# Three low parts of the first key's w1 go from GpSimd to VectorE, and the first tile's transposes all go inside the convolution (routed feed-forward, one core)

## Chip, cores and metric

The kernel runs on one core of a Trainium2 chip. The metric is the device time of one execution in microseconds (us). The time before is 1267.22 us, the median of three runs (1266.97 to 1270.43). The trace is of one further execution, profiled.

## What is computed

A causal seven-tap convolution with softmaxed taps is taken along the sequence for each head; its 28672 rows are then routed to eight experts. The routing is greedy over all (token, expert) logits in falling order, 3584 rows to an expert. Each expert is a feed-forward layer.

```python
w = softmax(weight)                              # 8 heads x 7 taps
x = conv(x_pad, w)                               # 28672 x 192, head by head
logits = x @ w_gate                              # 28672 x 8
assigned = greedy(logits, cap=3584)              # highest logits first
for e in range(8):
    h = maximum(x[assigned == e] @ w1[e], 0)     # w1: 192 x 1024
    out[assigned == e] = h @ w2[e]               # w2: 1024 x 192
```

## The kernel before

**Precision.** The matrix products of the feed-forward use a reduced float32 (`FR`) in two parts. A value is split into a high part, which ScalarE (ACT) copies, and a low part, the value less its high part, which a second engine subtracts. This holds for the weights (`wsplit`, L1208), for the transposed rows (`evac`, L1280) and for the hidden layer (`l1`, L1290: `hh` is high, `hl` is low).

**Convolution.** `moe_kernel` (L1420) loops over 16 blocks `i` of 1792 rows and, inside `k.conv` (L195), over eight heads `h`. The text calls one round of the inner loop step i.h; the planner's counter is `at = 8 * i + h`. Each step issues the convolution's matmuls for one head into one of four PSUM banks, then calls `mid(h)` (L1565), then lets ACT copy the bank into the block's tile `a`. After head 7 ACT's queue issues the store of the block to `attn` (L204). Inside `mid` a list `left` is worked off: VectorE transposes of the block before (`k.transp`, tile `aT`) and the gate's matmuls of the block before that (`gate`, then `end`, which ends in a maximum on VectorE, tile `M1`, printed as `M`). The gate needs all four transposes of its block.

**The first key.** A key is one expert's set of weights. From step 14.1 on, every odd step splits one piece of the first key's w1: a0 at 14.1, d0 at 14.3, a1 at 14.5, d1 at 14.7. A piece `a` is 128 x 512, a piece `d` is 64 x 512 (its load is two DMAs). `wsplit` has ACT make the high part, has the engine it is given make the low part, and then queues on SyncE (SP), in this order: a store of the high part (`kw`), a store of the low part (`kw` or `kd`, L1252), and the load of the piece four places further on (`wload`, L1190, tile `raw`). Four `raw` buffers circulate. The pieces behind d1 are the four w2 pieces of the first key, split in tile 0 of the feed-forward at f = 0 to 3, and a0, d0, a1, d1 of the second key, split at f = 4 to 7; their low parts are VectorE's.

**The first fetches.** When the first half of the routing is done, `hook` (L1539) calls `first()`, which queues on GpSimd (POOL) a memset and four indirect gathers for tile 0 and the same for tile 1 (`gather`, L1257, tile `xg`), and notes the step in `got`. From then on `mid` takes two items of `left` a step.

**The first tile's transposes.** `todo` (L1532) holds four items: the four TensorE transposes of tile 0's first 128 columns (u0) and their split into `xa`, then the four of the last 64 columns (u1) and their split into `xd`. `hook` takes two items in a step where `at >= got[0] + 10 and at % 8 in (2, 5)`; what is left is done behind the loop (L1589), ahead of the VectorE transposes of block 15 (L1591).

**Feed-forward.** `FFN.run` (L1384) goes through tiles of 512 rows. Per f, `l1` issues five matmuls into one of three banks `ph`; the first three read `xa`, the last two `xd`; ACT then writes `hh` and VectorE `hl`. Behind l1 of tile 0 stand, by `at(1)` (L1622), the gates and ends of blocks 14 and 15 (tile `bg` at this point), whose bias copies (`L`) are on ACT behind the last split of tile 0. Then tile 1 begins. Each engine takes its instructions in the order of the program; the order comes from a planner that adds up modelled engine times (`Pace`, L60).

```python
A.activation(hi, r, AF.Copy)
eng.tensor_tensor(lo, r[0:n], hi[0:n].bitcast(F32), op=OP.subtract)
...
S.dma_start(self.kept1[e][:, 2, s], hi.bitcast(F32))
S.dma_start(self.keptd[e][:, s], lo.bitcast(F32))
...
self.wload()
```

Of the kernel before, what the change touches and what calls it, by code (L numbers as in the profile page):

```python
# [1419 lines left out]
def moe_kernel(ctx, tc, x, weight, wg, w1, w2, out):  # L1420
    nc = Pace(tc.nc)
    V, P = nc.vector, nc.gpsimd
# [4 lines left out]
    with ExitStack() as cw:  # L1427
# [11 lines left out]
        ff = FFN(tc, nc, attn, w1, w2, out, r.ident, wr, drm)  # L1439
# [87 lines left out]
        def first():  # L1527
            for e in range(2):
                ff.gather(e, [ja0[:, e, b:b + 1] for b in range(4)], NTOK // 2, P)


        todo = [partial(f, 0, *a) for u in range(2) for f, a in ((lambda i, u: ff.transp(i, u, r.bg()), (u,)), (ff.evac, (u,)))]  # L1532
        got, left = [], []
# [5 lines left out]
        def hook(at):  # L1539
            nc.pe = max(nc.pe, PERIOD * at / 8 + START)  # L1540
            bg.hook(1.5)
            if not got and len(bg.gens) == 4:
                first()
                got.append(at)
            elif got and at >= got[0] + 10 and at % 8 in (2, 5) and todo:
                for _ in range(2):
                    todo.pop(0)()

# [5 lines left out]
        for i in range(NHB):  # L1554
            if i + 3 < NHB:
                k.load(i + 3)
            if i == 4:
                r.consts_late()
            if i == 13:
                cx[0].close()  # L1560
                for _ in range(4):
                    ff.wload()
                ff.wpool(cw, 0, **late)

            def mid(h):  # L1565

                if i and h == 0:
                    for u in range(4):
                        left.append(partial(k.transp, i - 1, u))
                        if i > 1:  # L1570
                            left.append(partial(gate, i - 2, u) if u < 3 else partial(end, i - 2))
                for _ in range(2 if got else 1):
                    if left and (i < LAG or got):
                        left.pop(0)()
                if i >= 14 and h % 2:
                    ff.wsplit(-1, P)
                hook(8 * i + h)

            k.conv(i, mid)
# [82 lines left out]
```

## Time and profile before

| what | value |
|---|---|
| median of three runs | 1267.22 us |
| profiled execution, its own time | 1268.0 us |
| span of the profiled execution | 1266.2 us |
| TensorE matmul (PE) busy | 1222.0 us, 97% of the span |
| VectorE (DVE) busy | 999.6 us, 79% |
| ACT busy | 551.2 us, 44% |
| POOL busy | 510.1 us, 40% |
| mean granted TensorE clock | 0.994 |

Times in the rows are us from the start of the span, durations of one instruction ns where the view says so. PEld is TensorE's weight load. SPq and ACTq are the DMA queues of SyncE and ScalarE. Most compute instructions show the one line L55, that of a helper, and are told apart by their tiles. A granted clock of 1.00 is 2.4 GHz, 0.50 is 1.2 GHz.

### The profile page before, as it was taken

What the parts mean: (1) busy time and instruction counts of PE and PEld (TensorE: products, weight loads), DVE (VectorE), ACT (ScalarE), POOL (GpSimd) and SP (SyncE); (2) the same over time, 40 slices, a digit from 0 to 9 for tenths busy, and PEclk for the clock granted to TensorE, in tenths of its full rate; (3) what the DMA queues carried; (4) which work ended last, traced back from release to release, by engine and by line L of the source; (5) the groups of instructions that cost most, each with busy time, mean ns of one, the idle gap of its engine ahead of it and who ended that gap; (6) DMA issues with size and microseconds to landing.
All of it is one profiled execution on the core that took longest, in us unless ns stands there. A gap on an engine that the chain in (4) does not pass through costs nothing.

```text
span 1266.2 us, 21792 instructions
## 1 busy us (share of the span) xinstructions
PE 1222.0 (97%) x7839; PEld 1049.9 (83%) x7839; DVE 999.6 (79%) x2245; ACT 551.2 (44%) x1220; POOL 510.1 (40%) x504
## 2 busy tenths in 40 slices
PE   5889979999999999999999999999999999999997
PEld 2445558899889888887889999999999999999997
DVE  7398669999999989988857777777777777777772
ACT  4544645565544543643433333333333333333332
POOL 3000435364444443533244444444444444444422
PEclk9999989999999999999999999999999999999999
DMA  9999897999533343423653513242314132231100
GB/s 236 347 334 297 271 328 257 294 316 319 194 103 112 122 152 94 152 93 125 161 126 105 205 41 100 94 155 62 129 48 147 46 102 97 85 105 47 45 26 28
DMA packets 100579, 193.02 MB, mean 152 GB/s; under 512 B 19232, under 2 KB 64752, under 8 KB 96240
## 3 DMA queue, kind: packets, MB, share of 16 engines
q1 hardware_dynamic: 57856, 115.15, 28.1%
q0 software_dynamic: 21504, 44.07, 11.7%
q10 hardware_dynamic: 21104, 32.34, 7.8%
q8 instruction: 63, 1.03, 0.3%
q14 instruction: 52, 0.43, 0.1%
HBM read 116.02 MB, written 75.50 MB: 151 GB/s over the span
## 4 chain that ended last, share of the span: by engine, by line
PE 83%; DVE 7%; DMA 5%; issue 1%; POOL 1%; ACT 1%; SPq 1%; POOLq 0%; ACTq 0%; DVEq 0%
PE ph L55 38%; PE y L55 37%; PE cv L55 3%; PE bg L55 3%; DMA X<-in_x_dram 1%; PE px L55 1%; DVE X L55 1%; DMA raw<-in_moe_w_dram 1%; DVE hl L55 1%; DVE oa L55 1%; DVE aT L55 1%; DMA wgr<-in_moe_w_gate_dram 1%; PE pl L55 1%; DMA X<-otab 1%; POOL xg L1262 0%
## 5 line engine op out<-in xcount | busy, mean ns | idle before, releaser
L55 PE MATMUL y<-w,hh 128*128 128x384 f32 x1792 | 539.3, 356 | 0.0
L55 ACT ACTIVATE hh<-ph 128x512 fp32r<-128x512 f32 x448 | 268.1, 598 | 494.2 <-PE ph L55 493.9
L55 PE MATMUL y<-w,hl 128*128 128x192 f32 x1792 | 448.9, 251 | 0.0
L55 DVE SCALAR_TENSOR_TENSOR hl<-ph,hh 128x512 fp32r<-128x512 f32 x448 | 308.1, 688 | 140.6 <-ACT hh L55 136.6
L55 PE MATMUL ph<-xa,w 128*128 128x512 f32 x1344 | 395.7, 402 | 3.9 <-DVE hl L55 3.9
L55 PEld LDWEIGHTS y<-w,hl 128*128 128x128 f32 x1792 | 341.0, 190 | 15.1
L55 PEld LDWEIGHTS y<-w,hh 128*128 128x128 f32 x1792 | 336.4, 188 | 19.1 <-issue 2.3
L1337 POOL DMA_INDIRECT out_dram<-yo,ib x128 | 127.9, 999 | 288.4 <-DVE yo L55 278.6
L55 PEld LDWEIGHTS ph<-xa,w 128*128 128x128 f32 x1344 | 218.7, 189 | 24.6 <-DVE hl L55 5.2
L1337 POOL DMA_INDIRECT out_dram<-yo,ia x96 | 112.2, 1168 | 262.3 <-DVE yo L55 230.0
L55 DVE STREAM_TRANSPOSE xs<-xg 32x256 f32<-32x256 f32 x496 | 182.9, 369 | 8.5
L55 PE MATMUL ph<-xd,w 128*128 128x512 f32 x448 | 177.3, 396 | 1.5 <-DVE xd L55 1.5
L55 PE MATMUL ph<-xd,dl 128*128 128x512 f32 x448 | 174.5, 390 | 0.0
L1262 POOL DMA_INDIRECT xg<-attn,jb x128 | 137.8, 1076 | 40.9 <-issue 40.9
L1262 POOL DMA_INDIRECT xg<-attn,ja x96 | 110.2, 1147 | 32.1 <-issue 26.7
L55 ACT ACTIVATE yt<-y 128x192 f32<-128x192 f32 x224 | 73.6, 328 | 102.6 <-PE y L55 99.5
L55 PE MATMUL cv<-X,TH 118*128 118x384 f32 x256 | 99.6, 515 | 18.9 <-DVE TH L55 12.5
L55 DVE TENSOR_TENSOR yo<-y,yt 128x192 f32<-128x192 f32 x224 | 79.4, 354 | 40.8 <-ACT yt L55 38.1
L55 PEld LDWEIGHTS ph<-xd,w 128*128 128x128 f32 x448 | 84.2, 188 | 21.2 <-DVE xd L55 2.0
L55 PEld LDWEIGHTS ph<-xd,dl 128*128 128x128 f32 x448 | 84.3, 188 | 19.7
L55 PEld LDWEIGHTS cv<-X,TH 118*128 118x128 f32 x256 | 44.6, 194 | 51.8 <-issue 13.0
L55 ACT ACTIVATE a<-cv 128x384 f32<-128x384 f32 x128 | 59.7, 492 | 53.3 <-PE cv L55 32.0
(237 smaller groups left out, 900.4 us busy)
## 6 DMA issues: line engine op xcount, KB each, us to landing
w<-kw SPq DMA_DIRECT2D x16, 1536.0 KB
w<-kv SPq DMA_DIRECT2D x16, 1536.0 KB
attn<-a ACTq DMA_DIRECT2D x16, 1344.0 KB
kw<-w SPq DMA_DIRECT2D x48, 256.0 KB
kv<-w SPq DMA_DIRECT2D x32, 384.0 KB
X<-in_x_dram SPq DMA_DIRECT2D x17, 672.0 KB
X<-in_x_dram ACTq DMA_DIRECT2D x15, 672.0 KB
raw<-in_moe_w_dram SPq DMA_DIRECT2D x32, 192.0 KB
```

The costliest lines, as they stand in the source:

```text
L55: return f(*a, **k)
L1262: self.nc.gpsimd.indirect_dma_start(out=t[:, b], out_offset=None, in_=self.attn[0:rows], in_offset=bass.IndirectOffsetOnAxis(ap=idx[b], ax ...
L1337: st = self.nc.gpsimd.indirect_dma_start(out=self.out, out_offset=bass.IndirectOffsetOnAxis(ap=idx, axis=0), in_=o, in_offset=None, bounds ...
```

## The change

The low parts of the first key's w1 are made by VectorE where the first fetches have already been queued, and by GpSimd otherwise. The condition for taking two items of `todo` becomes: at least 11 steps behind `got`, and an even counter.

```diff
@@ -1542,7 +1542,7 @@
             if not got and len(bg.gens) == 4:
                 first()
                 got.append(at)
-            elif got and at >= got[0] + 10 and at % 8 in (2, 5) and todo:
+            elif got and at >= got[0] + 11 and at % 2 == 0 and todo:
                 for _ in range(2):
                     todo.pop(0)()
 
@@ -1573,7 +1573,7 @@
                     if left and (i < LAG or got):
                         left.pop(0)()
                 if i >= 14 and h % 2:
-                    ff.wsplit(-1, P)
+                    ff.wsplit(-1, V if got else P)
                 hook(8 * i + h)
```

## Rows read from the trace of the kernel before

**Rows 1.** Page, part 1, busy time of TensorE (first of its lines)
```profile
PE 1222.0 (97%) x7839; PEld 1049.9 (83%) x7839; DVE 999.6 (79%) x2245; ACT 551.2 (44%) x1220; POOL 510.1 (40%) x504
```

**Rows 2.** Waits of TensorE from 185 us to the end, the longest kind: total, times, longest
```profile
PE bg L55 <- DVE c_bi L55: 2.0, 3, 1.0
```

**Rows 3.** Windows of 5 us; columns: length, busy PE, PEld, DVE, ACT, POOL, PEclk, DMA share, GB/s
```profile
155.00:160.00 5.00, 4.04 (x22) 2.43 (x18) 1.42 (x4) 3.46 (x9) 4.88 (x5) 1.00 0.55 159
160.00:165.00 5.00, 3.74 (x17) 2.84 (x18) 4.97 (x7) 2.95 (x6) 3.97 (x4) 1.00 1.00 304
...
175.00:180.00 5.00, 4.09 (x52) 2.73 (x50) 4.42 (x7) 3.57 (x7) 0.00 (x0) 0.50 1.03 384
```

**Rows 4.** Chain that ended last, 155 to 185 us: start, length, what
```profile
155.22 1.29 POOL dl L1243
...
174.15 5.30 DMA raw<-in_moe_w_dram
...
180.47 3.21 PE bg L55 x49
...
184.51 1.26 PE ph L55 x5
```

**Rows 5.** Waits of SP's queue, 100 to 215 us: total, times, longest
```profile
SPq L1252 <- POOL dl L1243: 9.6, 1, 9.6
```

**Rows 6.** Timeline of SP's queue: start, length, line, transfer
```profile
156.53 0.47 SPq L1252 DMA_DIRECT2D kd<-dl  x1
157.06 0.58 SPq L1203 DMA_DIRECT2D raw<-in_moe_w_dram  x1
...
162.53 2.54 SPq L1203 DMA_DIRECT2D raw<-in_moe_w_dram  x1
```

**Rows 7.** Timeline of ACT, 160 to 175 us: the idle time before and its releaser in brackets
```profile
168.29 0.53 ACT L55 ACTIVATE w<-raw 128x384 fp32r<-128x384 f32 x1 [3.13 <-DMA raw<-in_moe_w_dram]
...
172.09 0.52 ACT L55 ACTIVATE w<-raw 128x384 fp32r<-128x384 f32 x1 [2.78 <-DMA raw<-in_moe_w_dram]
```

**Rows 8.** Timeline of POOL, 140 to 175 us
```profile
141.82 1.28 POOL L1243 TENSOR_TENSOR w<-raw,w 128x512 fp32r<-128x512 f32 x1 [33.04 <-ACT w L55]
...
148.26 1.00 POOL L1262 DMA_INDIRECT xg<-attn,ja  x1 [0.30 <-issue]
...
172.26 1.00 POOL L1262 DMA_INDIRECT xg<-attn,ja  x1 [0.30 <-issue]
```

**Rows 9.** Instructions on tile raw, 100 to 190 us: min/median/max ns, first and last start
```profile
L55 DVE TENSOR_TENSOR dl<-raw,w x2: 683/683/683, 176.9 to 180.1; 64x512 fp32r<-64x512 f32 x2
```

**Rows 10.** Timeline of DVE, 150 to 175 us
```profile
151.33 0.38 DVE L55 TENSOR_REDUCE M<-LT 128x16 f32<-128x128 f32 x1 [1.17 <-ACT LT L55]
...
160.54 3.56 DVE L55 STREAM_TRANSPOSE aT<-a 128x768 f32<-128x768 f32 x4
...
172.64 0.56 DVE L55 TENSOR_TENSOR w<-raw,w 128x384 fp32r<-128x384 f32 x1 [2.61 <-ACT w L55]
```

**Rows 11.** Timeline of TensorE's weight loads, 154 to 157 us
```profile
154.97 0.30 PEld L55 LDWEIGHTS cv<-X,TH 118*128 118x128 f32 x2 [0.20 <-issue]
...
156.28 0.14 PEld L55 LDWEIGHTS bg<-ident,xg 128*128 128x128 f32 x1 [0.20 <-DMA xg<-attn,ja]
```

**Rows 12.** Tile xg, 100 to 200 us, last line: its 16 gathers from issue to landing
```profile
DMA to landing us min/median/max: 4.0/6.9/10.0
```

**Rows 13.** Timeline of TensorE, 156 to 176 us
```profile
156.45 1.46 PE L55 MATMUL cv<-X,TH 118*128 118x384 f32 x4
157.74 0.60 PE L55 MATMUL bg<-ident,xg 128*64 128x128 f32 x4
...
173.87 1.65 PE L55 MATMUL ph<-xa,w 128*128 128x512 f32 x3 [2.36 <-DVE hl L55]
```

**Rows 14.** Windows of 1 us around the change of clock; columns as in the windows of 5 us
```profile
173.00:174.00 1.00, 0.13 (x1) 0.13 (x1) 0.82 (x2) 0.09 (x1) 0.27 (x1) 0.61 0.93 348
...
183.00:184.00 1.00, 0.62 (x16) 0.20 (x4) 0.00 (x0) 0.30 (x2) 0.00 (x0) 0.77 1.04 369
```

## The prediction

> **What bounds the kernel now.** TensorE's matmuls are busy for 97% of the span [rows 1]. Behind 185 us the longest kind of wait that TensorE shows is 2.0 us in three waits [rows 2]: from there it runs nearly without a break. So whatever brings the start of tile 1 forward, or back, should reach the end one for one, and the reading turns to the stretch ahead of it. In the windows of 5 us the 16 DMA engines go from a share of 0.55 in 155 to 160 us to 1.00 and more behind it, while TensorE is not full [rows 3]. The chain of waits says what it stands on: a low part on POOL at 155.22, later a load of raw weights of 5.30 us that was issued at 174.15 (it lands at 179.45), then the last gates, then tile 1's first matmuls at 184.51 [rows 4]. The link between POOL and the loads is SP's queue. Its store of d0's low part waited 9.6 us for POOL [rows 5] and went out at 156.53; the loads of the second to the fourth w2 piece stand behind it, from 157.06 to 162.53 [rows 6]. ACT then waits 3.13 and 2.78 us for two of these, with the high parts of tile 0's hidden layer queued behind them [rows 7].
>
> **Part 1, three low parts on VectorE.** The first fetch stands behind POOL's a0 (141.82), the only split ahead of it [rows 8]: `got` is 113, step 14.1. So a0 stays on POOL, and d0, a1 and d1 move. VectorE takes 0.683 us for a 64 x 512 low part [rows 9]; a 128 x 512 one has as many columns, so the three cost 3 x 0.68 = 2.0 us. VectorE works in groups of four transposes and a maximum, with 1.17 us of idle time in front of the maximum [rows 10]. d0 fits into one group. a1 and d1, 1.4 us, meet in the next, and some 0.2 us of waiting for a1's high part comes on top: block 13's last transpose is 0.4 us late and the gate that needs it some 0.3 (bounds 0 and 0.7). This is hidden by the longer wait of part 2, and counts in full if that is gone.
>
> POOL is rid of three operations of 1.29 us [rows 4]. The next on its queue are a memset and the fetch for tile 2, which tile 1 needs; that gain is taken as nothing, with the whole of tile 0 as its cover.
>
> SP's store of d0 can go out 9.6 us earlier, at about 147, and the three loads behind it at about 147.5 to 151. ACT's two waits [rows 7] go. What is late next are the second key's loads, which SP issues only behind the stores of the w2 pieces in tile 0.
>
> While POOL issues the first four gathers, VectorE now has two low parts that read two SBUF tensors each. The rows show such a pair later: a gather issued at 172.26 takes the usual 1.00 us [rows 8] though a w2 low part of 0.56 us starts on VectorE at 172.64 [rows 10]. I add nothing. The Trainium skill (GPSIMD Engine Reference, Key points) says the opposite of such a pair: GpSimd shares its SBUF interfaces with VectorE and contends with VectorE instructions that have two SBUF inputs. By it the fetch would be held by up to two low parts, and the sum would be 1.4 us worse. The trace does not agree at the place just named.
>
> **Part 2, the transposes.** u0 moves from behind the convolution of step 15.5 to behind that of 15.4, u1 from behind the loop to behind that of 15.6. No matmul is added, but TensorE's order changes and with it what a late fetch holds up. Now u0's last block waits for `xg` and its weights are loaded at 156.28 [rows 11]; its gather was begun at 148.26 [rows 8], so it took 8.0 us. In the new order u0 would be asked for where the convolution of 15.5 was loaded, 154.97 [rows 11], with 0.3 us of part 1 on top. So TensorE waits at least 0.9 us, with three convolutions, ACT's copies of them and the last store to `attn` queued behind it.
>
> Call x the landing of that block. Behind it come its transpose (0.15), the convolution of 15.5 (0.65: two took 157.74 - 156.45 = 1.29 us [rows 13]), the end of block 13 (0.1), that of 15.6 (0.65) and u1 (0.36), then that of 15.7 (0.65) and ACT's split and two copies (some 1.2): x + 3.75. Then VectorE's four transposes of block 15, 3.56 us [rows 10]. Let T be their end, with which the hidden layer's low parts begin: T = x + 7.3. Now T = 160.54 + 3.56 = 164.10.
>
> What x is, no row shows. The lower end is 156.2, as now: T = 163.5, 0.6 earlier. But SP's stores and loads that went out from 156.5 on now come between 147 and 151: by the code's shapes 0.59 MB of loads and 1.05 MB of stores, 1.6 MB, which at 304 GB/s [rows 3] is 5.4 us of DMA time. The hole of 155 to 160 (5 x 0.45 = 2.25 us) takes less than half of that, so the engines stay full for about 3 us longer. In the full stretch gathers needed up to 10.0 us [rows 12], which gives x = 158.3. I take 157.8, nearer to this end because the engines will be full: T = 165.1, **1.0 us later**.
>
> **Part 3, from T to tile 1.** With the w2 pieces there, VectorE has four `hl`, four w2 low parts and one of `xa` ahead of SP's last store of w2: nine instructions of 0.56 to 0.68 us, 5.5 us. SP then issues that store and the load of d1's two halves, 0.8: T + 6.3 instead of 174.15 = T + 10.05. Lands after 5.30 us as now [rows 4]: T + 11.6 = 176.7 instead of 179.45, **2.75 us earlier**. From the landing to tile 1 it is 184.51 - 179.45 = 5.06 us: a split, a bias copy, gates, a copy, a transpose.
>
> Those gates run at half clock, 3.21 us [rows 4]. The granted clock fell in the window from 173 to 174, behind an idle time of 2.36 us that ends at 173.87 [rows 13], and rose in that from 183 to 184 [rows 14]. In the new order TensorE is done with tile 0 some 4 us earlier and then waits about 3 us for d1, longer than 2.36; I take the same 5.06 us. Bounds: 1.6 us less, if the 3.21 us are halved at full clock; 1.9 more, if the low clock lasts 10 us as now, from about 175.5 to 185.5, over 3.75 us of tile 1.
>
> **Sum.** Profiled execution 1268.0 - 2.75 = 1265.25. It lies 0.78 above the median of the runs shown, so the forecast is **1264.5**.
>
> **Rivals.**
> R1, the fetch lands as now (x = 156.2). T = 163.5, d1 at 175.1, 4.35 us earlier; with the second gates on average in the middle of their clock's bounds 1.0 more: 5.35, **1261.9**. For it: the gathers are issued before most of the added transfers. Against: gathers of 10.0 us in the full stretch [rows 12].
>
> R2, the loads are hidden anyway. The DMA engines are full from 160 on [rows 3], and the same bytes have to pass ahead of d1; if the stalled TensorE issues block 15's store to `attn` 3 us later, the hole is only moved and d1 lands at 179.45 as now: 0, **1267.2**. Against it: bytes issued behind d1's load also fill that stretch.
>
> R3, slower: the fetch becomes the bound. Its gathers share the engines with ACT's store and now SP's transfers too. If the slowest gather, 10.0 us [rows 12], needs half as long again, 15 us from 148.26, then x = 163.3, T = 170.6, d1 lands at 182.2, 2.75 us later: **1270.0**. It decides from x = 160.6 on, where d1 lands as now. Of such sharing the Trainium skill (DMA: Bandwidth & Descriptors, Queues, rings and completion order) says that each DMA engine goes round the queue rows with work, packet by packet; no row here shows the queues' turns.
>
> R4, VectorE's low parts hold the fetch: 1.4 us on x, so the gain falls to 1.35: **1265.9**. Only the skill's sentence in part 1 speaks for it.
>
> That the change does nothing is excluded: all of its steps lie in 14.3 to 15.6 and `got` is 113.
>
> **How the numbers follow.** Forecast 0.38, R1 0.27, R2 0.18, R3 0.12, R4 0.05. A measurement of this kernel can tell about 0.3%, 3.8 us, from no change. Faster by more (under 1263.4) is most of R1 and a tenth of the forecast's spread: 0.30. Slower by more (over 1271.0) is the upper part of R3 and a little for an order of work not seen here: 0.09. The rest, 0.61, is within. The range reaches from below R1 (with the gates wholly at full clock, 0.6 less, and 0.8 for the spread between runs) to most of the way to R3: 1260.5 to 1269.0.
>
> **What would show it.** On the new profile: `kd` out near 147 and no wait of SP for POOL; no wait of ACT for w2's loads in tile 0; a wait of TensorE's weight load for `xg` in block 15, which gives x; T from the four transposes; d1's issue and landing; the granted clock behind it; tile 1's first matmul, whose shift should be the whole difference. The forecast is wrong if x lies under 157 or over 160, if d1's load is issued as forecast and lands no earlier, or if TensorE shows new waits behind tile 1.

## The result, and the profile after

The changed kernel took 1270.99 us (median of 22 runs, 1267.5 to 1276.44), the kernel before, beside it, 1267.88 us (22 runs, 1266.25 to 1273.83). The ratio is 1.0023 with a 95% interval of 1.0014 to 1.0032: slower, by 0.23%, within the 0.3% that the prediction called no change, but slower where its 1264.5 us was faster, and above its range of 1260.5 to 1269.0 us. The profiled execution took 1269.41 us (span 1267.6), 1.4 us more than the one of before. The runs below come in five sets (e1 to e4; the two e0, e5, e6; e7 to e10; e11 to e14; e15, e16), in which the kernel before took 1276.8, 1272.9, 1275.3, 1269.1 and 1269.2 us (medians), so a kernel is compared inside its set alone.

Timeline of SP's queue after the change, the answer to [rows 5, 6]:

```profile
146.79 0.47 SPq L1252 DMA_DIRECT2D kd<-dl  x1
147.32 0.59 SPq L1203 DMA_DIRECT2D raw<-in_moe_w_dram  x1
...
150.29 2.74 SPq L1251 DMA_DIRECT2D kw<-w  x1
153.12 1.86 SPq L1252 DMA_DIRECT2D kd<-dl  x1
155.03 2.34 SPq L1203 DMA_DIRECT2D raw<-in_moe_w_dram  x1
...
175.06 1.60 SPq L1201 DMA_DIRECT2D raw<-in_moe_w_dram  x1
```

The first half of the plan worked. d0's store goes out at 146.79 instead of 156.53, the last load of the first key at 155.03 instead of 162.53 (the prediction had some 151), and ACT's waits for w2 in tile 0 [rows 7] are gone. But the last load of the second key, which is what the forecast lived on, starts at 175.06 and not earlier than the 174.15 of before [rows 4].

The reason is on TensorE (timeline; in brackets the idle time before and its releaser), the answer to [rows 11, 13]:

```profile
155.13 0.55 PE L55 MATMUL bg<-ident,xg 128*128 128x128 f32 x3
159.75 0.48 PE L55 MATMUL bg<-ident,xg 128*128 128x128 f32 x1 [4.08 <-DMA xg<-attn,ja]
160.02 1.49 PE L55 MATMUL cv<-X,TH 118*128 118x384 f32 x2
```

Three gathered blocks are there at 155.13. The fourth is waited for until 159.75, 4.08 us, with three convolutions and the last store behind it. The chain of waits after the change runs through the same place:

```profile
146.98 1.51 POOL xg L1262
148.80 10.91 DMA xg<-attn,ja
```

The gather that starts at 148.80 lands 10.9 us later; before it started at 148.26 and landed after 8.0 us [rows 8, 11]. The third gather takes 1.51 us; before it took 1.00 (timeline of POOL before the change):

```profile
146.96 1.00 POOL L1262 DMA_INDIRECT xg<-attn,ja  x1 [0.30 <-issue]
```

Windows of 5 us of the changed kernel, columns as in [rows 3]:

```profile
155.00:160.00 5.00, 0.92 (x12) 0.56 (x5) 0.00 (x0) 0.43 (x2) 0.73 (x1) 0.93 0.98 301
160.00:165.00 5.00, 4.95 (x16) 2.78 (x16) 2.75 (x5) 2.98 (x7) 1.96 (x3) 0.73 0.08 30
...
180.00:185.00 5.00, 2.76 (x46) 2.36 (x49) 2.11 (x4) 1.42 (x5) 0.00 (x0) 0.50 1.03 371
```

The hole in the transfers is not filled, it has moved: the DMA share is now 0.98 from 155 to 160 us and 0.08 from 160 to 165, where it was 0.55 and 1.00 [rows 3]. TensorE works 0.92 us in the first of these windows and comes out of it at a granted clock of 0.73 in the next, part of it (160 to 162 us) at 0.50: the two passes of a convolution take 1.49 us at 160.02, and 0.81 us at 163.18, when the clock is back.

What the end of tile 0 makes of it, timeline of TensorE:

```profile
182.24 0.47 PE L55 MATMUL bg<-ident,L 128*128 128x128 f32 x1 [5.05 <-ACT L L55]
182.65 2.79 PE L55 MATMUL bg<-aT,c_mu 128*32 128x128 f32 x48
...
186.20 1.10 PE L55 MATMUL ph<-xa,w 128*128 128x512 f32 x3
```

Tile 1's first matmul stands at 186.20; before the change the same timeline has it behind the gates at 184.40 (the chain, [rows 4], counts it from 184.51):

```profile
184.40 0.93 PE L55 MATMUL ph<-xa,w 128*128 128x512 f32 x3
```

The loss is 1.8 us at this point and 1.4 at the end. In between it moves: the scatters of `out` on POOL stand 2.0 us later than before at 191 us, 2.7 at 263 and 1.6 from 661 us on. The gates before tile 1 run at half clock (2.79 us), as before.

### The profile page after: what moved, and what is told of

The parts are those of the page before. It is cut to its first block, busy times and chain, and to the rows that moved or that the text cites. A ratio compares the mean times of both kernels' runs of the same rounds, so it can differ in the third digit from the quotient of the medians.

```text
span 1267.6 us, 21799 instructions
## 1 busy us (share of the span) xinstructions
PE 1222.3 (96%) x7839; PEld 1050.0 (83%) x7839; DVE 1000.8 (79%) x2248; ACT 550.3 (43%) x1220; POOL 506.6 (40%) x501
## 4 chain that ended last, share of the span: by engine, by line
PE 83%; DVE 8%; DMA 5%; issue 2%; ACT 1%; SPq 1%; POOL 1%; POOLq 0%; ACTq 0%; DVEq 0%
PE ph L55 38%; PE y L55 37%; PE cv L55 3%; PE bg L55 2%; DMA X<-in_x_dram 1%; PE px L55 1%; DVE oa L55 1%; DVE X L55 1%; DVE hl L55 1%; DVE aT L55 1%; DMA wgr<-in_moe_w_gate_dram 1%; DMA xg<-attn,ja 1%; PE pl L55 1%; DMA kv<-w 1%; DMA raw<-in_moe_w_dram 1%
## 5 line engine op out<-in xcount | busy, mean ns | idle before, releaser
L55 PE MATMUL cv<-X,TH 118*128 118x384 f32 x256 | 102.3, 525 | 17.1 <-DMA X<-in_x_dram 13.6
```

Source lines behind the costliest of these rows:

```text
L55: return f(*a, **k)
```

## Experiments

### The halves alone, and other places for the transposes

The first two kernels (e1, e2) each take one line of the change into the kernel before. The low parts alone:

```diff
-                    ff.wsplit(-1, P)
+                    ff.wsplit(-1, V if got else P)
```

> Only the low parts go to VectorE; the transposes stay where they were (u0 behind 15.5, u1 behind the loop). Theory A (SP's stores and loads, now out 10 us earlier, starve the fetch, and TensorE in its order holds the convolution for it): the fetch's last block lands near 159.5 us again instead of 156.2, TensorE waits 3 to 4 us for it at u0, T (end of block 15's VectorE transposes, 164.1 before) is 167 to 168, and the time is 1 to 3 us above the kernel before. Rival C (the earlier place of the transposes is what costs): no loss, or 2 to 4 us faster than before.

Measured: ratio 0.9993 (0.9974 to 1.0011).

The transposes alone:

```diff
-            elif got and at >= got[0] + 10 and at % 8 in (2, 5) and todo:
+            elif got and at >= got[0] + 11 and at % 2 == 0 and todo:
```

> Only the transposes move; the low parts stay on GpSimd. Theory A: the fetch lands at 156.2 as before, TensorE waits about 1 us for it behind step 15.4, T is 163.5 to 164.2 and the time lies within 1 us of the kernel before. Rival C: most of the 3.1 us loss is here.

Measured: ratio 1.0012 (0.9994 to 1.0030). In this profile, with POOL's low parts kept, the eight transposes went through at 156.54 and 158.44 without a wait for the fetch, and w2's loads stayed at 157.19 to 161.38.

Neither half can be told from nothing. In the profile of e1 TensorE also stood 2.39 us ahead of a logit transpose at 153.79, for nothing that the trace names, so its profile decides nothing either.

The next kernel (e4) keeps the low parts on VectorE and puts all eight transposes behind the loop, behind VectorE's transposes of block 15:

```diff
-            elif got and at >= got[0] + 11 and at % 2 == 0 and todo:
+            elif False:
...
-        for f in left + todo:
+        for f in left:
             f()
         for u in range(4):
             k.transp(15, u)
+        for f in todo:
+            f()
```

> The low parts on VectorE as in the change, but all eight transposes of tile 0 behind the loop, and behind block 15's VectorE transposes. Theory A: the fetch still lands near 159.7, but the convolution and block 15's store no longer wait for it (store near 157.5 instead of 164.8), the hole in the DMA between 160 and 165.5 is gone, T is near 161.5, tile 1 starts near 181 and the time is 1264 to 1265.5, below both kernels. Rival R2 (the same bytes have to pass, so d1 lands as before): tile 1 starts at 184 or later and the time is that of the kernel before, 1267 to 1268.

Measured: ratio 1.0002 (0.9986 to 1.0019). The transposes stand at 161.06, tile 1 at 186.11. A place that waits for no fetch gives the time back as a later start of tile 0.

### Holding SP's transfers back

In e3 the changed kernel's stores of d0, a1 and d1 and the loads behind them go on a list in `wsplit`, which is worked off behind the convolution's loop:

```diff
+        if self.hold is not None:
+            self.hold.append(lambda: self.keep(S, what, e, s, t, hi, lo))
+            self.done += 1
+            return
...
+        for f in ff.hold:
+            f()
```

> The change, with the stores and loads that SP makes for d0, a1 and d1 queued only behind the convolution loop; VectorE's low parts stay where the change has them. Theory A: the fetch lands at 156.2 to 156.8, TensorE waits about 1 us, T is 163.5 to 164.5, and with the loads as late as before the time is within 1 us of the kernel before. Rival B (VectorE's low parts with two SBUF inputs hold GpSimd's fetch): the fetch lands near 159.7 all the same and the time is 2 to 5 us above before.

Measured: ratio 1.0001 (0.9979 to 1.0022). A miss in its design: nothing else stood on SP's queue, so a later place in the program changed no transfer (d0's stores and the loads go out as in the changed kernel, the first load at 147.71), and the run is one more of the change. So in e5 a small store that waits for block 13's maximum stands ahead of the list:

```diff
+        nc.sync.dma_start(drm.tile([128, 16], F32, name="late"), r.M1[:, 208:224])
         for f in ff.hold:
             f()
```

> The change, with an 8 KB store of block 13's maximum put on SP's queue ahead of the stores and loads for d0, a1 and d1, so that these go out behind step 15.5 as in the kernel before (deferring them in the program alone left SP's queue as it was, since nothing else stood on it). VectorE's low parts stay. Theory A: the fetch lands at 156 to 157 and TensorE's wait for it is about 1 us; the time is within 2 us of the kernel before. Rival B (VectorE's low parts hold GpSimd's gathers): the fetch lands near 159.7 as in the change.

Measured: ratio 1.0018 (1.0004 to 1.0032), slower. Now w2's loads go out from 163.16 and no fetch was waited for (fourth gather at 150.89, transposes of u0 at 157.93 and 158.66), but tile 1 came at 187.56. Holding loads and stores together gives up what the change was for. So the next step parts the two.

### The stores alone

In e6 the changed kernel stores the first key's w1 parts (1.57 MB by the shapes) behind tile 0's loads instead of at once:

```diff
         S = self.nc.sync
+        if i < 0:
+            def put():
+                if what == "a":
+                    S.dma_start(self.kept1[e][:, 0, s], hi.bitcast(F32))
...
+            self.puts.append(put)
...
             if i == 1:
+                for put in ff.puts:
+                    put()
                 bg.drain(3)
```

The second set ran it beside both kernels.

> The kernel before, unchanged, for a profile on the same chip as the next three: the fetch lands near 156 us if this chip is like the first one; every theory expects the time of the kernel before.

> The change, unchanged, on the same chip as the next two. Theory A (SP's earlier transfers starve the fetch; TensorE holds the convolution and block 15's store for it) expects the fetch at 159 to 160 us and tile 1 about 2 us later than in the kernel before; time 1 to 4 us above it.

> The change, with the eight stores of the first key's w1 (1.57 MB) queued on SP behind tile 0's loads; the loads stay early. Theory A: with 1.3 MB less ahead of it the fetch lands at 154 to 156, T is near 163, the second key's d1 lands near 173 to 175, tile 1 starts near 179 to 181 and the time is 3 to 5 us below the kernel before. Rival R2 (only the sum of the bytes counts, wherever they stand): tile 1 at 184 or later and no gain.

Measured: before 1271.62 us in a single run, tile 1 at 184.59; the change 1.0002 (0.9987 to 1.0018), tile 1 at 183.13; stores late 0.9995 (0.9979 to 1.0010), tile 1 at 182.98. So here the change brought tile 1 forward by 1.5 us, with no wait for the fetch, and yet ended 1.3 us later in the span. The lead of 0.9 us in the scatters of `out` from 191 us on is held until 475; it is lost where VectorE stood 0.99 and 1.40 us, and another 1.0 us around 650. For the 0.99 us the trace names nothing, for the 1.40 us TensorE's `ph`; why these waits are longer than in the kernel before stays open. Theory and result did not meet, and whether the late fetch belongs to the change was open again.

### The clock ahead of the gates

In e9 spare transposes into an unread part of the bank stand ahead of the logit transposes of blocks 14 and 15, to keep TensorE at work; e10 is the changed kernel, unedited, beside it.

```diff
         pt = k.bank("pt")
+        if i >= 14:
+            for _ in range(14):
+                PE.transpose(pt[:, 128:256], k.ident, k.ident)
         PE.transpose(pt[:, 0:128], L, k.ident)
```

> The changed kernel with 14 spare 128x128 transposes on TensorE ahead of each of the two logit transposes of blocks 14 and 15, in the stretch where it stood for 5.05 us and its clock fell to 0.50. Theory (the half clock behind that idle time costs the gates 2.8 instead of 1.5 us and tile 1's first matmuls 0.4 us): the granted clock stays at 1.00 between 165 and 190 us, the second gates take about 1.5 us, tile 1 comes about 1.7 us earlier than in the changed kernel, ratio about 0.998 to 0.999. Rival (the clock falls all the same or tile 1 waits for the load): the spare transposes only add up to 3 us to the gates' chain, ratio 1.000 to 1.002.

> The changed kernel itself, for a profile and a ratio on the chip of these runs. If its loss of 0.23% holds on every chip: ratio 1.001 to 1.003. If what it gains and loses about tile 0 hangs on where the fetch lands and the clock falls on that chip, as the second chip's 1.0002 suggests: 0.999 to 1.001.

Measured: with the spare transposes 1.0011 (0.9999 to 1.0024), the change beside it 1.0020 (0.9998 to 1.0041). The second gates of the kernel with the spare transposes:

```profile
182.78 1.68 PE L55 MATMUL bg<-aT,c_mu 128*32 128x128 f32 x48
```

They take 1.68 us, near full clock, against 2.67 in e10, and the mean granted clock of the 12 runs is 0.9942 against 0.9923. But from the landing (ACT's copy of d1) to tile 1 it is 187.46 - 181.52 = 5.9 us, against 183.89 - 179.05 = 4.8 in e10. So the clock was kept for the gates (0.90 from 180 to 185 us, 0.71 in e10; behind them it is 0.76 and 1.00), but at this point the spare matmuls cost 1.1 us more than it gave, and the two ratios can't be told apart. In the profile of e10 no fetch is waited for: the fourth gather begins at 148.33, and the four transposes of u0 run from 157.58 without a break.

### Is the late fetch the change's?

Two more profiles of the change and one of the kernel before, all unedited, in one set:

> The changed kernel, one more profile. If the fetch lands late because of the earlier transfers: TensorE waits 3 us or more for the fourth gathered block and starts tile 0's transposes at 159 us or later, as in the first profile. If that was one execution's or one chip's: no wait over 1 us, transposes by 158 us. In either case tile 1's first ph 5.0 us behind the landing of the second key's last load.

> The kernel before, one more profile: TensorE's wait for the fourth gathered block under 1 us, end of block 15's transposes at 164 to 165 us, second key's last load landing at 179.5 us, tile 1 at 184.5 us.

> The changed kernel once more, as the other repeat: what differs between the two repeats is the scatter of executions, and what both share against the kernel before is the change's.

Measured: change 1272.30 and 1270.56 us, before 1266.22, one run each. The timeline of POOL in the second repeat of the change (e14), third and fourth gather:

```profile
147.22 1.52 POOL L1262 DMA_INDIRECT xg<-attn,ja  x1 [0.30 <-issue]
149.04 1.00 POOL L1262 DMA_INDIRECT xg<-attn,ja  x1 [0.30 <-issue]
```

That of VectorE, with the low part of a1:

```profile
147.17 0.69 DVE L55 TENSOR_TENSOR w<-raw,w 128x512 fp32r<-128x512 f32 x1 [0.20 <-ACT w L55]
```

That of ACT's queue, with block 14's store:

```profile
148.87 0.31 ACTq L204 DMA_DIRECT2D attn<-a  x1
```

And that of TensorE, with the transpose that waits for the fourth gather:

```profile
160.17 0.33 PE L55 MATMUL bg<-ident,xg 128*128 128x128 f32 x1 [4.25 <-DMA xg<-attn,ja]
```

In the kernel before (e13) the timeline of the weight loads has that transpose here:

```profile
156.24 0.14 PEld L55 LDWEIGHTS bg<-ident,xg 128*128 128x128 f32 x1 [0.28 <-DMA xg<-attn,ja]
```

So the late fetch was no accident of the first profile: 160.17 - 149.04 = 11.1 us here, 162.60 - 151.68 = 10.9 in the other repeat, 10.9 in the first profile, against 156.24 - 148.15 = 8.1 in e13 and 8.0 in the first profile of before. But the change does not always have it. In the second set (the change again) POOL, ACT's queue and TensorE show:

```profile
148.35 1.00 POOL L1262 DMA_INDIRECT xg<-attn,ja  x1 [0.30 <-issue]
150.51 0.31 ACTq L204 DMA_DIRECT2D attn<-a  x1
156.48 0.65 PE L55 MATMUL bg<-ident,xg 128*128 128x128 f32 x4
```

The four transposes run through without a wait, so the fourth gather landed within some 8.5 us; e10 has no such wait either. In these two ACT's store of block 14 goes out 2.2 and 1.5 us behind the fourth gather, in the three late ones 0.17 us ahead of it. Tile 1 in e14 and in e13:

```profile
186.89 1.50 PE L55 MATMUL ph<-xa,w 128*128 128x512 f32 x3
183.15 1.26 PE L55 MATMUL ph<-xa,w 128*128 128x512 f32 x3
```

They are 3.7 us apart. In e12, where all work from the first gather on stands 2.9 us later than in the first profile, it starts at 188.93.

### Gates ahead of the loads

In every profile so far tile 1 stood 4.0 to 5.9 us behind ACT's copy of d1 (4.0 in e5, 4.4 in e13), though its first four f need nothing of d1. The gates' copies simply stand behind that copy in ACT's queue. The edit, in e7 on the changed kernel and in e8 on the one before, puts the gates and ends of blocks 14 and 15 behind l1 of tile 0 at f = 3 to 5:

```diff
+        def early(f):
+            if 3 <= f < 6 and len(bg.gens) == 4:
+                bg.run(1 if f == 5 else 3)
...
                 if i < n:
+                    if not i:
+                        self.early(f)
                     self.wsplit(i, eng(f))
```

> The changed kernel, with the gates and logit rows of blocks 14 and 15 put into the program behind the first layer of tile 0's pieces 3 to 5, ahead of the second key's loads on ScalarE, instead of behind tile 0. Theory (tile 1 stands 5 us behind the landing of the second key's last load because the gates' copies are queued behind that load's copy on ScalarE): tile 1's first ph comes within 2 us of that landing instead of 5.0 us, so about 3 us earlier than in the changed kernel on the same chip, and the time falls by as much: ratio about 0.997 to 0.998. Rival (what is gained at tile 1 is lost again behind it, as 1.5 us of lead were on the second chip): tile 1 starts earlier by 3 us and the ratio still is 0.999 to 1.001. Second rival (tile 1 is held by something else, its own gathers or tile 0's hh): tile 1 starts where it did.

> The same edit in the kernel before, without the change. Theory: tile 1's first ph within 2 us of the landing of the second key's last load, about 3 us earlier than in the kernel before, ratio about 0.997 to 0.998, the same gain as in the changed kernel, so that the change's own worth beside it stays within 0.1%. Rival: the ratio stays at 0.999 to 1.001.

Measured: 1.0009 (0.9991 to 1.0028) in the changed kernel, 0.9993 (0.9979 to 1.0007) in the one before. Both times ACT stood ahead of block 15's logit copy for something that the trace doesn't name (timeline of ACT, e7):

```profile
176.94 0.22 ACT L55 ACTIVATE L<-bg 128x64 f32<-128x64 f32 x1 [5.75 <-remote]
```

The matmuls that it reads had ended at 172.8, and the program has it wait for TensorE alone; so the edit was neither shown nor refuted. In the fourth and fifth set it was run together with the late stores of e6, in e11 on the changed kernel and in e15 on the one before; e16 is e6 again:

> The changed kernel with both edits: the first key's w1 stores behind tile 0's loads, and the gates of blocks 14 and 15 ahead of the second key's loads. Theory (the second key's last load, and behind it the gates, set tile 1's start): that load lands at about 178 us and tile 1's first ph follows within 2 us, at about 180 us, 3 us earlier than with the stores moved alone; ratio 0.997 to 0.999. Rival (ScalarE stands about 5 us ahead of block 15's logit copy, as it did in both kernels with the gates first, for something the trace doesn't name): tile 1 comes at 182 us or later and the ratio is 0.999 to 1.001.

> The kernel before, without the change, with both edits of the version that was 0.45% faster (first key's w1 stores behind tile 0's loads, gates of blocks 14 and 15 ahead of the second key's loads). If the two edits made that gain: ratio 0.995 to 0.997. If the change has its share in it, once its stores no longer stand between the gathers' packets (w2's loads at 145 instead of 157 us, second key's last load landing 2 us earlier): ratio 0.997 to 0.999, some 2 us slower than that version.

> The changed kernel with the stores moved alone, once more, on the chip of the other run. If the stores made the gather late: TensorE's wait for the fourth gathered block under 1.5 us instead of 4.0 to 4.3, tile 1 at 183 us or earlier, ratio 0.997 to 0.9995. If the gates' place is what counts: tile 1 within 1 us of the kernel before, ratio 0.999 to 1.001.

| kernel | median us | before beside it | ratio (95%) |
|---|---|---|---|
| change, stores late (e16) | 1267.56 (12 runs) | 1269.21 (23) | 0.9989 (0.9978 to 1.0001) |
| change, stores late, gates first (e11) | 1263.47 (6) | 1269.12 (11) | 0.9955 (0.9938 to 0.9972) |
| before, stores late, gates first (e15) | 1264.32 (12) | 1269.21 (23) | 0.9963 (0.9947 to 0.9980) |

The timeline of POOL in e16, where the stores alone were moved, fourth gather:

```profile
151.84 1.00 POOL L1272 DMA_INDIRECT xg<-attn,ja  x1 [0.30 <-issue]
```

And of TensorE:

```profile
159.49 0.33 PE L55 MATMUL bg<-ident,xg 128*128 128x128 f32 x1 [0.78 <-DMA xg<-attn,ja]
```

With the stores gone from there the fourth gather lands after 159.49 - 151.84 = 7.7 us (e11: 158.16 - 150.45 = 7.7), and TensorE waits 0.8 us instead of 4, though the gather begins 0.18 us behind ACT's store as in the late profiles, and the third gather takes 1.51 us. With that order, then, the w1 stores are what makes the fetch late, shown by taking them away; w2's loads go out just as early in these kernels. What the late fetch costs in time is not shown apart: no set has a series of runs of the change with it beside one without it.

The timeline of TensorE in e11, second logit transpose and tile 1:

```profile
172.72 0.33 PE L55 MATMUL bg<-ident,L 128*128 128x128 f32 x1 [0.55 <-ACT L L55]
...
176.78 0.96 PE L55 MATMUL ph<-xa,w 128*128 128x512 f32 x3 [0.30 <-DVE hl L55]
```

The same two in e15:

```profile
171.35 0.27 PE L55 MATMUL bg<-ident,L 128*128 128x128 f32 x1
...
173.77 0.84 PE L55 MATMUL ph<-xa,w 128*128 128x512 f32 x3
```

The waits of 4 to 5 us ahead of the logit transposes are gone, and tile 1 starts at 176.78 and 173.77 instead of 183.15 (e13), 2.2 and 3.3 us ahead of ACT's copy of d1 (178.97 and 177.03): it did not need d1. The windows of e15 show TensorE at full clock through the stretch:

```profile
165.00:170.00 5.00, 5.00 (x108) 3.93 (x106) 4.27 (x9) 2.26 (x6) 1.00 (x1) 1.00 0.89 302
170.00:175.00 5.00, 5.00 (x29) 3.84 (x22) 3.42 (x7) 4.28 (x10) 3.28 (x3) 1.00 0.93 296
175.00:180.00 5.00, 5.00 (x30) 4.38 (x30) 4.28 (x8) 2.28 (x5) 0.00 (x0) 1.00 1.03 402
```

In the first profile of before, the last of these stood at a clock of 0.50 [rows 3]. Both kernels beat the one before by 0.4%, and the change's two single runs in the fourth set (1272.30 and 1270.56 us) by more. Not all of the 9.4 us between e13 and e15 come through: the spans are 1.5 us apart, the medians of the kernel before and of e15 4.9. The first scatter of `out` is 8.3 us earlier in e15 (181.71 and 190.00), those from 660 us on 1.4; between 185 and 230 us the windows have TensorE idle for 5.0 us in e15 and 0.7 in e13. Each span is of one execution, and e13's has a mean granted clock of 0.998. That of the timed runs is 0.9957 in e15 and 0.9932 in the kernel before beside it.

The change adds nothing here that could be measured: the intervals of 0.9955 and 0.9963 overlap. What the gates' place brings without the stores' was run in e7 and e8 alone, and stays open.

## Why the prediction was wrong

Part 1 was right but for the pair on POOL and VectorE and the last load's issue (155.03). The chain of parts 2 and 3 had the right links, and four of them were sized too short:

| term | forecast | profile of the change | repeat e14 |
|---|---|---|---|
| x, landing of the fourth block | 157.8 | 159.75 | 160.17 |
| T - x | 7.3 | 8.56 (T = 164.75 + 3.56) | 8.63 |
| T to the issue of d1's last load | 6.3 | 6.75 (175.06) | 6.98 |
| issue to landing (ACT's copy of d1) | 5.30 | 6.18 (181.24) | 6.15 |
| landing to tile 1 | 5.06 | 4.96 (186.20) | 4.96 |

The differences are 1.95 + 1.26 + 0.45 + 0.88 - 0.10 = 4.44 us. The forecast had tile 1 at 184.51 - 2.75 = 181.76; with them it is the 186.20 of the profile. So **the step that failed is the size of x**, the landing of the fourth block, taken as 157.8 with an upper end of 158.3; it was 159.75, and behind it T - x and the load's time to land were sized too short by 1.26 and 0.88 us. The upper end took 10.0 us of gather time from [rows 12]. That view knows the landing of four of the sixteen gathers only (5.0, 4.0, 10.0 and 8.7 us), and the 10.0 is a gather for tile 2, begun just behind the store of d1's low part (POOL and SP's queue before the change):

```profile
160.12 1.02 POOL L1262 DMA_INDIRECT xg<-attn,ja  x1 [0.16 <-issue]
160.11 2.36 SPq L1252 DMA_DIRECT2D kd<-dl  x1
```

It was one row of a stretch with stores in it, and not a bound. The fourth gather took 10.9, and itself began 0.54 us later.

- **Part 1, low part beside gather.** "I add nothing" for the pair of low part and gather was wrong. The third gather took 1.51 or 1.52 us in all five profiles in which VectorE's low part of a1 began 0.05 us ahead of it (147.17 against 147.22 in e14), and 1.00 us in the nine profiles of the first three sets in which VectorE makes that low part, where it began some 0.15 us behind it. The place that I had named, 172.64 against 172.26, was of the second kind. So these profiles agree with what the Trainium skill (GPSIMD Engine Reference, Key points) says of contention, and the row did not speak against it; the price was 0.51 us, not 1.4. Rival R4's mechanism fits at a third of its size; no run moved this low part alone.
- **Behind that half microsecond stands an order.** The fourth gather now begins 0.17 us behind ACT's store of block 14 (149.04 and 148.87 in e14); before it began 0.34 us ahead of it (148.26 and 148.60). In e16 and e11 it begins 0.17 to 0.18 us behind that store too and lands after 7.7 us, so this order alone does not make it late; with the w1 stores it does. Where it began ahead of the store in spite of the w1 stores (the change in the second set) it landed within some 8.5 us. That both are needed fits all profiles, but no run parted the order from the rest.
- **R3, the fetch becomes the bound,** was right in its cause and had a chance of 0.12. Its point of decision, x = 160.6, was put too high because the other terms were too short: in the profile d1 landed at 181.24, 1.79 behind the 179.45 of before, so with the measured terms it lies at 159.75 - 1.79 = 158.0, close to the x that I took. Bytes by queue from 150 to 156 us before (packets, MB, share of 16 engines):

```profile
q10 hardware_dynamic: 427, 1.26, 62.5%
q0 software_dynamic: 199, 0.41, 21.3%
```

And in the changed kernel:

```profile
q10 hardware_dynamic: 397, 1.22, 62.4%
q1 hardware_dynamic: 516, 0.69, 34.3%
q0 software_dynamic: 75, 0.16, 6.7%
```

The gathers' queue (q0) moves 0.16 MB instead of 0.41 while SP's (q1) moves 0.69; ACT's store (q10) loses 0.04 MB. The Trainium skill (DMA: Bandwidth & Descriptors, Queues, rings and completion order) has each engine go round the queue rows with work, packet by packet. Here the gathers' queue lost 62% of its packets and ACT's 7%, where an even turn would take from both; whether the gathers' queue had work all the time, no row shows.

- **R2, the hole is only moved,** is what the windows show: block 15's store went out at 164.75 instead of 158.85, behind the hole. d1's load left 0.9 us later than before, not 2.75 earlier, because T, on which its issue hangs, was 168.31 and not 165.1.
- **T - x** was worked out at full clock. Behind 4 us of idle time the two convolutions, the transposes and the copies that wait for them ran in part at 0.50 (two passes in 1.49 and 1.39 us instead of 0.81).
- **Landing to tile 1** was right to 0.1 us, at half clock. That this term is no property of the load, but of where the gates stand in ACT's queue, I had in the rows and did not ask; e11 and e15 show it.
- **"One for one".** That tile 1's shift reaches the end in full was the first premise. In the first profile 1.8 us became 1.4; in the second set the change had tile 1 1.5 us earlier and ended 1.3 us later; e15 kept 1.5 of 9.4. So even with x as early as in the second set, at 156.5, the time did not fall (1.0002).
- **Slips in the sums,** on which little hangs: of the stores that SP sent out from 156.5 on there were 0.92 MB and not 1.05, as d0's high part had gone out at 145.83; and R1's further 1.0 us does not follow from the bounds of 1.6 less and 1.9 more.
- **The sum against the median.** The profile is 1.4 us slower, the medians 3.1. The profiled execution, at a mean granted clock of 0.994, lies 1.6 us below the median of the changed kernel, whose 22 runs have 0.9918. For the runs of the kernel before beside them no clock is on record; in the later sets it has 0.9932 to 0.9938. A mean lower by 0.0015 would be 0.003 of the 1268 us more at half clock, 3.8 us, in which TensorE does the work of 1.9. That this makes up the rest is argued, not shown, and the loss is not the same in every set: 1.0023 here, 1.0001 in e3, 1.0002 in the second set and 1.0020 (0.9998 to 1.0041) in the third.

## What to carry to other kernels

Transfers that come early are not free because they are off the path: ask which fetch they will share the engines with, and move only the ones that someone waits for; here the stores, sent early, made a fetch late in three of five profiles of the change, and the loads alone did not. Where a long wait in front of a tile ends with a load, look whether the tile needs that load, or whether something it does need stands behind it in a queue: reordering that, together with the later stores, was worth 0.4%, with the change or without it. A price taken from the slowest row of a trace is no upper bound for a stretch that the trace doesn't hold.

## What the runs showed of the hardware

- A gather that POOL begins 0.05 us behind a VectorE subtraction of two SBUF tensors took 1.51 us, one that had begun some 0.15 us ahead of it 1.00 us; the loss was there in five profiles of five, and in none of nine.
- The same 128-row gather landed 10.9 to 11.1 us from its start where it began 0.17 us behind ACT's store of a block and SP had w1 stores queued in these microseconds (three profiles), and after 7.7 us with the same order and no such stores (e11, e16); ahead of ACT's store it took 8.0 and 8.1 us without them and no more than some 8.5 with them.
- Time and mean granted clock go together within one kernel, whichever causes the other: of the changed kernel's 22 runs the slowest at 0.988 took 1276.4 us, the one at 0.995 took 1267.5 us.
- ACT stood 5.75 us in e7 and 4.82 us in e8 ahead of a copy for which, by the program, it waits for TensorE alone, whose matmuls had ended; in e11 and e15 it did not. What it stood for is open.
